# Attention plus maxout experts on one core: reordered first loads, one store per output tile, and column tiles for the last 64 queries

## The chip, the cores and the metric

The kernel runs on one core of a Trainium2 chip. The metric is the device time of one execution in microseconds (us). The kernel before the change takes 385.0 us (median; 383.74 to 385.46). "Ratio" below is the mean time of one kernel's fast runs over the mean of the other's of the same rounds, so it is not quite the ratio of the medians that are quoted; the bracket after it is its 95% interval. "Faster" or "slower" means by more than 2%.

Names used: PE is the matrix engine and PEld its weight load; ACT, DVE and POOL are the scalar, vector and general engines; SPq is the queue of SyncE, which issues nearly all transfers. "exp" is one ACT instruction, on 128x1024 elements in 312 of the 336 cases and on fewer in the rest.

## The reference, cut to what matters

```python
# q, k, v: [B=8, H=8, S=1152, D=64] float32
q_pool = q.reshape(B, H, S // 2, 2, D).mean(axis=3)            # 576 queries
scores = (1 / sqrt(D)) * q_pool @ k.transpose(0, 1, 3, 2)
attn = exp(scores - max) / sum                                 # softmax over 1152 keys
x = (attn @ v).transpose(0, 2, 1, 3).reshape(4608, 512)
g = maximum(x @ w1, x @ w2)                                    # [4608, 1024]
out = g @ w_out                                                # [4608, 512] float32
```

## The kernel before

The kernel is written as its own scheduler. `Plan` holds a planned clock for every engine. Jobs (transposes, attention products, expert products) offer *units* to PE, and a loop picks the next unit by planned times. The result is one fixed instruction order for each engine, and PE runs it in that order. So each planned cost (`cost=`) decides the order, and a wrong one can show as a wait on the chip.

Work is done for pairs of heads, 32 pairs in all. Scores for a pair use two row tiles of PE (64 contraction rows each). The attention-value product has the exponentials `et` as stationary operand and `vE` (64 values and a column of ones) as the moving one, so 65 columns stream for each 128 queries. 576 queries are four and a half chunks of 128: the last 64 queries were padded to 128 columns.

```python
def chunk(half, sb):                       # half: head of the pair; sb: 0..4
    def go(e, m):
        for t in range(NT):                # 9 key blocks
            a = (half * 2 + es) * PW + t * SQ + sb * P
            last = e.matmul(fb[m][:, sb*66:sb*66+65], et[:, a:a + P],
                            vE[vs][:, t, half, 0:65], start=(t == 0), stop=(t == NT-1))
        return last
    return unit(need, 0.275, go)
# norm(half): one reciprocal [128 x 5], one multiply [128 x 5 x 64] into xnat
return [Job("a", [chunk(half, sb) for sb in range(NCH + 1)], norm(half), nb=i) for half in range(2)]
```

The expert part transposes x (`xT`) by transfers for most batches, by PE for the first and the last (`X_PE = (0, B - 1)`), computes `h` jobs (four matmuls of 512 columns each) and `p` jobs (twelve), and stores tiles of 128 tokens. Token order inside a tile is two groups of 64 rows, and each group lands in rows of `out` that are nine apart:

```python
def store(lo, s):                                   # before: two transfers per tile
    for half in range(2):
        n0 = lo + half * HP                         # HP = 64
        b, at = n0 // SQ, n0 % SQ
        if b % 2: at = (at - NB) % SQ
        op("SP", lambda e, b=b, u=at // HP, half=half: e.dma_start(
            out[b*SQ:(b+1)*SQ, :].rearrange("(p u) e -> u p e", u=QU)[u, :, :],   # 64 x 512
            osb[s][rows(half), :]), r=[f"osb{s}"], dma=f"d_o{s}", cost=0.4)
```

The planned cost of an exp is `0.24 + n/700` for n columns of a head, 0.971 us for the usual 512. Bursts of scores hold 2 or 3 exps' worth; the third is allowed while the expert backlog is over 600 tokens (`LAG`).

The softmax here doesn't subtract the row's maximum and nothing guards it: scores larger than these inputs give would overflow.

Of the kernel before, what the change touches and what calls it, by code (L numbers as in the profile page):

```python
# [7 lines left out]
P = 128  # L8
# [7 lines left out]
class Plan:  # L16
# [29 lines left out]
    def when(self, eng, r=(), w=(), after=()):  # L46

        t = self.free.get(eng, 0.0)
        for d in self.deps(r, w, after)[0]:
            p = self.ops[d]  # L50
            if p["eng"] != eng or p["dma"] is not None:
                t = max(t, p["seen"] + 0.05)
        return t

    def op(self, eng, fn, r=(), w=(), dma=None, cost=0.1, mode="f", after=(), solo=False):
# [9 lines left out]
        if dma is not None:  # L65
            self.free[eng] = t + (1.3 if mode == "t" else 0.5)
            self.dma_free = max(self.free[eng] + 1.2, self.dma_free) + cost
            seen = self.dma_free + 0.7
        else:
            if eng == "PE" and mode != self.mode:  # L70
                t += 0.1
                self.mode = mode
            self.free[eng] = t + cost
            seen = t + cost + self.LAT[eng]
# [9 lines left out]
    def solve(self):  # L84
# [3 lines left out]
        for n, o in enumerate(ops):  # L88
# [3 lines left out]
            for d in sorted(o["deps"], reverse=True):  # L92
                p = ops[d]
                if p["dma"] is None:
                    if p["eng"] == eng and (eng == "PE" or d not in o["raw"]):
                        continue
# [57 lines left out]
def bass_funnel_attn__then__act_maxout2_kernel(  # L154
# [32 lines left out]
    with ctx:  # L187
# [10 lines left out]
        qp = [sbuf([HP, QU, 2, D], BF16, f"qp{s}") for s in range(2)]  # L198
# [4 lines left out]
        et = sbuf([P, 4 * PW + HP], BF16, "et")  # L203
        et2 = et[:, 0:4 * PW].rearrange("p (h c) -> p h c", h=2)
# [25 lines left out]

        def setup():
# [5 lines left out]
            def ones(g):  # L237
                g.memset(et[:, 4 * PW:], 0.0)
# [4 lines left out]
            op("POOL", ones, w=["vE0", "vE1", "vE2", "pad"])  # L243

        def load_k(i, lo=0, hi=NT):
            b, h0, s = i // NHP, 2 * (i % NHP), i % 3
            op("SP", lambda e: e.dma_start(
                kraw[s][:, :, lo:hi, :],
                k[b, h0:h0 + 2, :, :].rearrange("h (p t) d -> p h t d", t=NT)[:, :, lo:hi, :]),
                w=[f"kraw{s}"] if hi == NT else [f"kraw{s}.0"], dma=f"d_k{s}" if hi == NT else "d_k",  # L250
                cost=1.5 * (hi - lo) / NT)

        def load_q(i):
            b, h0, s = i // NHP, 2 * (i % NHP), i % 3
            for half in range(2) if i == 0 else (None,):
                at = slice(0, P) if half is None else rows(half)
                hs = slice(h0, h0 + 2) if half is None else slice(h0 + half, h0 + half + 1)
                op("SP", lambda e, at=at, hs=hs: e.dma_start(
                    qraw[s][at, :, :, :].rearrange("p u r d -> p (u r d)"),
                    q[b, hs, :, :].rearrange("h (p r) d -> (h p) (r d)", p=HP)),  # L260
                    w=["qraw0.0"] if half == 0 else [f"qraw{s}"],
                    dma="d_q" if half == 0 else f"d_q{s}", cost=1.45 if half is None else 0.75)
# [8 lines left out]
        def cast_k(i):  # L271
# [4 lines left out]
                w=[f"kbf{s}"] + (["kbf0.0", "kbf0.3"] if i == 2 else []), cost=1.13)  # L276

        def cast_k0(lo, hi, part):
            op("ACT", lambda e: e.activation(
                kbf[0][:, lo:hi, :, :].rearrange("p t h d -> p h t d"), kraw[0][:, :, lo:hi, :],  # L280
                COPY), r=[part], w=[f"kbf0.{lo}"], cost=0.2 + (hi - lo) * 0.092)
# [10 lines left out]

        def cast_q(i):
            s, r = i % 2, i % 3
            for half in range(2):
                a = qraw[r][rows(half), :, :, :]
                op("DVE" if i == 0 else "POOL", lambda g, half=half, a=a: g.tensor_tensor(  # L297
                    qp[s][:, :, half, :], a[:, :, 0, :], a[:, :, 1, :], ALU.add),
                    r=["qraw0.0" if i == 0 and half == 0 else f"qraw{r}"], w=[f"qp{s}.{half}"], cost=0.65 if i == 0 else 1.4,
                    solo=i > 0 and half == 1)  # L300

        def cast_v(i):
# [3 lines left out]
                1.0, 1.0, ALU.mult, ALU.mult), r=[f"vraw{r}"], w=[f"vE{r}"], cost=1.13)  # L306

        def unit(r, cost, go, mode="f"):
# [3 lines left out]
            return r, plan_it, cost  # L312
# [4 lines left out]
        def qtrans(i):  # L317
# [10 lines left out]
            def evac(m):  # L328
                mb = fb[m][:, :].bitcast(BF16)
                dve(lambda e: e.tensor_copy(qpT[i % 3][:, :], mb[:, 0:SQ]),  # L330
                    [f"f{m}"], [f"qpT{i % 3}", f"f{m}"], 0.4)
            return Job("q", [unit([f"qp{s}.0", f"qp{s}.1", "ident"], 0.3, go, "s")], evac, ("q", i))

# [7 lines left out]
        def ktrans_pe(i, cuts=(0, 5, 9)):  # L341
# [3 lines left out]
            for lo, hi in zip(cuts, cuts[1:]):  # L345
# [8 lines left out]
                def evac(m, lo=lo, hi=hi):  # L354
# [4 lines left out]
                        [f"f{m}"], kkeys(i, lo, hi) + [f"f{m}"], 0.1 + (hi - lo) * 0.12)  # L359
# [5 lines left out]
        def av_jobs(i):  # L365
# [5 lines left out]
            need = [f"et{es}.{g - first(i)}" for g in range(first(i), after(i))] + [f"vE{vs}", "pad"]  # L371

            def chunk(half, sb):

                def go(e, m):
                    for t in range(NT):
                        a = (half * 2 + es) * PW + t * SQ + sb * P
# [5 lines left out]

            def norm(half):
                def evac(m):
                    c = c0 + half * D
                    a = fb[m][:, 0:(NCH + 1) * 66].rearrange("p (j c) -> p j c", c=66)
                    dve(lambda e: e.reciprocal(rc[half][:, :], a[:, :, 64:65]),  # L388
                        [f"f{m}"], [f"rc{half}"], 0.19)
                    dve(lambda e: e.tensor_tensor(  # L390
                        xnat[xs][:, :, c:c + D], a[:, :, 0:D],
                        rc[half][:, :].unsqueeze(2).to_broadcast([P, NCH + 1, D]), ALU.mult),
                        [f"f{m}", f"rc{half}"],
                        [f"xn{xs}.{h0 + half}", f"f{m}"], 0.5)
                return evac

            return [Job("a", [chunk(half, sb) for sb in range(NCH + 1)], norm(half), nb=i)
                    for half in range(2)]
# [21 lines left out]
        def skeys(g):  # L420
            return [key for i, t, *_ in pieces(g) for key in (f"kT{i % 3}.{t}", f"qpT{i % 3}")]

        def scores(g):
# [10 lines left out]
            def exp(a, z, keys):  # L434
# [3 lines left out]
                    r=[f"s{r}"], w=keys + [f"s{r}"], cost=0.24 + (z - a) / 700.0)  # L438
# [20 lines left out]
        def under(n0, n1):  # L459

            keys = [key for key, lo, hi in (("w2b", 512, 1536), ("w2T", 1536, 2560),
                                            ("w2f", 2560, NTOK)) if n0 < hi and lo < n1]
            if "w2T" in keys:
                keys += [f"w2T{ct}" for ct in range(NC_)]
            return keys

        def xsize(j):
            return P if j < NCH else NB

        def xtrans(b):  # L470
            xs = b % 2
            assert b == 0 or not queue["w"]
            for j in range(NCH + 1):
# [3 lines left out]
                    r=[f"xn{xs}.{h}" for h in range(H)], w=xkeys(n0, n0 + n),  # L477
                    after=under(n0, n0 + n), dma=f"d_x{xs}{j}", cost=0.65, mode="t")

        def xtrans_pe(b):  # L480
            xs = b % 2
            jobs = []
            for j in range(NCH + 1):
# [14 lines left out]
                jobs.append(Job("x", [unit([f"xn{xs}.{h}" for h in range(H)] + ["ident"],  # L498
# [15 lines left out]
        def w_cast(part, ct):  # L514
            if part == 0:
                dve(lambda e: e.tensor_copy(w2b[:, ct, :], w2f[:, ct, :]),
                    [f"w2f{ct}"], [f"w2b{ct}", "w2b"], 0.6)
            elif part == 1:
                dve(lambda e: e.tensor_tensor(  # L519
                    wd[:, ct, :], w1f[:, ct, :], w2f[:, ct, :], ALU.subtract),  # L520
                    [f"w1f{ct}", f"w2f{ct}"], [f"wd{ct}", "w2f"], 1.2)
            else:
                dve(lambda e: e.tensor_copy(  # L523
                    wo[:, 2 * ct:2 * ct + 2, :], wof[:, 2 * ct:2 * ct + 2, :]),
                    [f"wof{ct}"], [f"wo{2 * ct}", f"wo{2 * ct + 1}"], 0.6)

        def w2t_job(ct):
# [7 lines left out]
            def evac(m):  # L535
# [3 lines left out]
                    [f"f{m}"], [f"w2T{ct}", "w2T", f"f{m}"], 1.15)  # L539
            return Job("w", [unit([f"w2b{ct}", "w2b", "ident"], 0.44, go)], evac)  # L540
# [19 lines left out]
        def store(lo, s):  # L560

            for half in range(2):
                n0 = lo + half * HP
                b, at = n0 // SQ, n0 % SQ
                if b % 2:
                    at = (at - NB) % SQ
                op("SP", lambda e, b=b, u=at // HP, half=half: e.dma_start(
                    out[b * SQ:(b + 1) * SQ, :].rearrange("(p u) e -> u p e", u=QU)[u, :, :],
                    osb[s][rows(half), :]), r=[f"osb{s}"], dma=f"d_o{s}", cost=0.4)
# [4 lines left out]
        def h_jobs(nb, tail):  # L574
# [4 lines left out]
            for ft in range(NF):  # L579
# [6 lines left out]
                def evac(m, ft=ft):  # L586
# [5 lines left out]
                    else:  # L592
                        dve(lambda e: e.tensor_scalar_max(  # L593
                            gT[:, ft, g0:g0 + size], fb[m][:, 0:size], 0.0),
                            [f"f{m}"], w, 0.1 + size / 960.0)
# [3 lines left out]
        def p_job(lo, tail):  # L599
            hi = lo + P  # L600

            def part(j):
                def go(e, m):
# [5 lines left out]
                    return e.matmul(fb[m][:, :], lhs, rhs, start=(j == 0), stop=(j == NC_ + NF - 1))  # L609
                if j < NC_:  # L610
                    return unit([f"w21{j}"] + xkeys(lo, hi), 0.216, go)
                return unit([f"wo{j - NC_}", f"gT.{lo % RING // P}.{j - NC_}"], 0.216, go)

            def evac(m):
                o = ocount[0] % 4
# [6 lines left out]
                else:  # L622
                    dve(lambda e: e.tensor_copy(osb[o][:, :], fb[m][:, :]),  # L623
                        [f"f{m}"], [f"osb{o}", f"f{m}"], 0.63)
                held[o] = (lo, o)
            return Job("p", [part(j) for j in range(NC_ + NF)], evac, nb=hi)
# [11 lines left out]
        p_got = set()  # L638
        p_at = [0]
# [53 lines left out]
        def start_w(n):  # L693
            for ct in range(NC_):
                load("w", (n, ct), got_w, f"{('w2f', 'w1f', 'wof')[n]}{ct}")

        def got_w(at):
# [3 lines left out]
            def ready():  # L701
# [3 lines left out]
                elif n == 2 and ct == NC_ - 1:  # L705
# [18 lines left out]
        def flush():  # L724
# [24 lines left out]
            for b in list(x_wait):  # L749
# [3 lines left out]
                elif plan.ops[plan.writer[f"xn{b % 2}.{H - 1}"]]["seen"] <= now():  # L753
# [15 lines left out]
        def burst_size():  # L769

            done = [b for b in range(B) if all(av_half.get(b * NHP + j) == 2 for j in range(NHP))]
            return 3 if len(done) * SQ - p_end[0] > LAG else 2

        def more_moe():
# [10 lines left out]
            while p_at[0] + P <= h_end[0] and f"w21{NC_ - 1}" in plan.writer:  # L785
                queue["p"].append(p_job(p_at[0], tail))
# [58 lines left out]
        def emit_unit(kk):  # L845
# [17 lines left out]
            elif job.kind == "p":  # L863
                p_got.add(job.nb)
                while p_end[0] + P in p_got:
                    p_end[0] += P
            if job.done:
# [7 lines left out]

        setup()
        load_q(0)
        load_k(0, 0, 3)
        load_k(0, 3, NT)
        cast_k0(0, 3, "kraw0.0")  # L880
        cast_q(0)
        cast_k0(3, NT, "kraw0")
        queue["q"].append(qtrans(0))
        queue["k"].extend(ktrans_pe(0, (0, 3, NT)))
        load_k(1)
        load_q(1)
        load_v(0)
        cast_k(1)
        queue["k"].extend(ktrans_pe(1))
        cast_q(1)  # L890
        queue["q"].append(qtrans(1))
        cast_v(0)
        load("k", 2, load_k, "kraw2")
        load("q", 2, load_q, "qraw2")
# [98 lines left out]
```

## Time and profile before

| | before |
|---|---|
| time, median | 385.0 us |
| span in the profile | 382.8 us |
| PE busy | 363.7 us, 95% |
| ACT busy | 316.9 us, 83% |
| mean DMA rate | 231 GB/s |

Two stretches of the same kernel. Columns: stretch, length, then busy us (and count) of PE, PEld, DVE, ACT, POOL, then granted PE clock, DMA share, GB/s.

```profile
20.00:40.00 20.00, 16.43 (x334) 11.76 (x333) 12.09 (x24) 18.93 (x23) 11.41 (x9) 1.00 1.04 396
...
200.00:220.00 20.00, 20.00 (x293) 12.01 (x293) 6.01 (x13) 18.88 (x22) 9.41 (x9) 1.00 1.11 309
```

Early on ACT leads (18.93 of 20 us); from about 60 us to 340 us PE has almost no gaps.

Two of the waits (total us, times, longest), and two steps of PE in order of time (start, us, what):

```profile
POOL qp L297 <- DMA qpT<-qp: 21.3, 13, 4.3
...
PEld sps L429 <- ACT et L436: 15.3, 37, 0.8
```

```profile
120.47 0.83 PE L429 MATMUL sps<-qpT,kT 64*128 64x320 bf16 x12
...
121.23 1.53 PE L378 MATMUL fb<-vE,et 128*128 128x65 bf16 x45
```

The 45 matmuls of the second step are one head's five chunks of nine; single records in it start 29 ns apart.

### The profile page before, as it was taken

The numbers are of one execution on the slowest core, as the hardware profiler recorded it, in microseconds if no ns is written. First come the engines' busy times: TensorE is split into PE (matmuls) and PEld (weight loads), VectorE is DVE, ScalarE is ACT, GpSimd is POOL, SyncE is SP. The second block draws the span as 40 slices with busy tenths as digits, with TensorE's granted clock in tenths as the row PEclk, the third lists the DMA queues.
The fourth block names the chain that finished last, engine by engine and source line by source line (L and its number), as shares of the span: only waits on it lengthen the run. The fifth ranks groups of instructions, "written<-read, shape, count | busy, mean of one in ns | idle before, by whom it ended". The sixth has DMA issues, their size and how long they took to land.

```text
span 382.8 us, 11318 instructions
## 1 busy us (share of the span) xinstructions
PE 363.7 (95%) x5010; PEld 210.8 (55%) x5010; DVE 140.2 (37%) x283; ACT 316.9 (83%) x355; POOL 162.0 (42%) x135
## 2 busy tenths in 40 slices
PE   2787999999999999999999999999999999999995
PEld 1365546555555555455556565555455655667642
DVE  2274934442234223422252224422442244237201
ACT  3998989999999999999999999999899999902210
POOL 1955597665554555555453535545545110000000
PEclk9999999999999999999999999999999999999999
DMA  8999999999989998999799999999899460121144
GB/s 248 405 391 399 392 257 312 331 309 312 225 234 295 273 272 174 309 320 275 142 265 289 319 179 212 286 258 315 200 236 267 94 109 14 29 44 42 29 95 98
DMA packets 93521, 88.58 MB, mean 231 GB/s; under 512 B 66080, under 2 KB 66592, under 8 KB 93472
## 3 DMA queue, kind: packets, MB, share of 16 engines
q1 hardware_dynamic: 93472, 87.86, 89.4%
q8 instruction: 39, 0.64, 0.7%
q14 instruction: 10, 0.08, 0.1%
HBM read 62.91 MB, written 9.44 MB: 189 GB/s over the span
## 4 chain that ended last, share of the span: by engine, by line
PE 85%; DMA 6%; DVE 4%; POOL 2%; issue 1%; SPq 1%; POOLq 0%
PE fb L378 22%; PE fb L609 21%; PE sps L429 18%; PE fb L582 15%; PE sps L609 4%; DMA qraw<-in_q_dram 3%; DMA kraw<-in_k_dram 2%; PE sps L582 2%; DVE wd L519 2%; POOL qp L297 1%; PE fb L547 1%; DVE xnat L390 1%; POOL vE L304 1%; PE fb L489 1%; DVE wo L523 1%
## 5 line engine op out<-in xcount | busy, mean ns | idle before, releaser
L436 ACT ACTIVATE et<-sps 128x1024 bf16<-128x1024 f32 (+1 forms) x336 | 307.8, 1005 | 19.0 <-PE sps L429 17.2
L378 PEld LDWEIGHTS fb<-vE,et 128*128 128x128 bf16 x2880 | 93.4, 97 | 20.9 <-issue 10.9
L378 PE MATMUL fb<-vE,et 128*128 128x65 bf16 x2880 | 101.9, 193 | 0.3
L297 POOL TENSOR_TENSOR qp<-qraw 64x576 bf16<-64x576 f32 x62 | 88.6, 1429 | 30.6 <-DMA qpT<-qp 21.3
L429 PE MATMUL sps<-qpT,kT 64*128 64x512 bf16 (+7 forms) x1152 | 96.9, 289 | 3.0 <-ACT et L436 2.1
L304 POOL TENSOR_SCALAR vE<-vraw 128x1152 bf16<-128x1152 f32 x32 | 36.9, 1152 | 103.2 <-PE fb L378 95.8
L429 PEld LDWEIGHTS sps<-qpT,kT 64*128 64x128 bf16 x1152 | 41.8, 95 | 51.3 <-issue 19.6
L582 PE MATMUL fb<-xT,wd 128*128 128x512 bf16 (+3 forms) x276 | 63.1, 360 | 0.7 <-DVE stage L623 0.7
L609 PE MATMUL fb<-wo,stage 128*128 128x512 bf16 x240 | 62.4, 380 | 0.0
L593 DVE TENSOR_SCALAR stage<-fb 128x512 bf16<-128x512 f32 (+3 forms) x64 | 41.9, 657 | 32.3 <-PE fb L582 32.1
L388 DVE RECIPROCAL rc<-fb 128x5 f32<-128x5 f32 x64 | 12.4, 194 | 112.3 <-PE fb L378 112.3
L273 POOL TENSOR_SCALAR kbf<-kraw 128x1152 bf16<-128x1152 f32 x31 | 36.2, 1167 | 14.6 <-DMA kraw<-in_k_dram 12.5
L582 PEld LDWEIGHTS fb<-xT,wd 128*128 128x128 bf16 x276 | 22.8, 98 | 29.4 <-DVE stage L593 6.3
L623 DVE COPY stage<-fb 128x512 f32<-128x512 f32 x29 | 20.0, 690 | 50.2 <-PE fb L609 49.7
L609 PEld LDWEIGHTS fb<-wo,stage 128*128 128x128 bf16 x240 | 21.1, 97 | 23.3 <-issue 3.3
L390 DVE TENSOR_TENSOR xnat<-fb,rc 128x320 bf16<-128x320 f32 x64 | 31.5, 491 | 2.2
L609 PE MATMUL fb<-w,xT 128*128 128x512 bf16 x120 | 32.1, 380 | 0.0
L609 PEld LDWEIGHTS fb<-w,xT 128*128 128x128 bf16 x120 | 10.3, 98 | 11.7 <-issue 2.0
L589 ACT ACTIVATE stage<-sps 128x256 bf16<-128x256 f32 (+1 forms) x7 | 2.3, 338 | 16.4 <-PE sps L582 16.4
L620 ACT COPY stage<-sps 128x512 f32<-128x512 f32 x3 | 1.8, 585 | 13.8 <-PE sps L609 13.8
L609 PE MATMUL sps<-wo,stage 128*128 128x512 bf16 x48 | 11.3, 379 | 0.0
L582 PE MATMUL sps<-xT,wd 128*128 128x256 bf16 (+2 forms) x76 | 10.3, 275 | 0.0
(40 smaller groups left out, 96.4 us busy)
## 6 DMA issues: line engine op xcount, KB each, us to landing
vraw<-in_v_dram SPq DMA_DIRECT2D x32, 576.0 KB, 7.7
kraw<-in_k_dram SPq DMA_DIRECT2D x31, 576.0 KB, 6.6
qraw<-in_q_dram SPq DMA_DIRECT2D x31, 576.0 KB, 5.8
out_dram<-stage SPq DMA_DIRECT2D x72, 128.0 KB, 2.4
xT<-in_moe_w_dram SPq DMA_DIRECT2D x4, 512.0 KB, 11.9
stage<-in_moe_w_out_dram SPq DMA_DIRECT2D x4, 512.0 KB, 14.2
stage<-in_moe_w_dram SPq DMA_DIRECT2D x4, 512.0 KB, 13.2
qraw<-in_q_dram SPq DMA_DIRECT2D x2, 288.0 KB, 4.1
```

Source lines behind the costliest of these rows:

```text
L273: op("POOL", lambda g: g.tensor_scalar(kbf[s][:, :, :, :].rearrange("p t h d -> p h t d"), kraw[r][:, :, :, :], 1.0, 1.0, ALU.mult, ALU.mu ...
L297: op("DVE" if i == 0 else "POOL", lambda g, half=half, a=a: g.tensor_tensor(qp[s][:, :, half, :], a[:, :, 0, :], a[:, :, 1, :], ALU.add), ...
L304: op("POOL", lambda g: g.tensor_scalar(vE[r][:, :, :, 0:D].rearrange("p t h d -> p h t d"), vraw[r][:, :, :, :], 1.0, 1.0, ALU.mult, ALU.m ...
L378: last = e.matmul(fb[m][:, sb * 66:sb * 66 + 65], et[:, a:a + P], vE[vs][:, t, half, 0:65], start=(t == 0), stop=(t == NT - 1))
L388: dve(lambda e: e.reciprocal(rc[half][:, :], a[:, :, 64:65]), [f"f{m}"], [f"rc{half}"], 0.19)
L390: dve(lambda e: e.tensor_tensor(xnat[xs][:, :, c:c + D], a[:, :, 0:D], rc[half][:, :].unsqueeze(2).to_broadcast([P, NCH + 1, D]), ALU.mult ...
L429: last = e.matmul(sps[r][:, h, col:col + hi - lo], kT[i % 3][rows(h), t, :], qpT[i % 3][rows(h), lo:hi], start=True, stop=True)
L436: op("ACT", lambda e: e.activation(et2[:, :, c:c + z - a], sps[r][:, :, a - g * W:z - g * W], EXP, scale=scale), r=[f"s{r}"], w=keys + [f" ...
L582: return e.matmul(fb[m][:, 0:size], wd[:, ct, ft * P:(ft + 1) * P], xT[:, ct, n0:n1], start=(ct == 0), stop=(ct == NC_ - 1))
L593: dve(lambda e: e.tensor_scalar_max(gT[:, ft, g0:g0 + size], fb[m][:, 0:size], 0.0), [f"f{m}"], w, 0.1 + size / 960.0)
L609: return e.matmul(fb[m][:, :], lhs, rhs, start=(j == 0), stop=(j == NC_ + NF - 1))
L623: dve(lambda e: e.tensor_copy(osb[o][:, :], fb[m][:, :]), [f"f{m}"], [f"osb{o}", f"f{m}"], 0.63)
```

## The change

The change has four intentions:

1. The last 64 queries of the two heads of a pair, padded to 128 columns before, run as two *column tiles*: each stationary block has 64 columns and sits in one half of PE's columns, so the two heads' products can run at the same time.
2. An output tile is stored with one transfer instead of two; the last tile is split by columns, 384 and 128.
3. The first loads are reordered and cut differently (q in two pieces, k whole).
4. The planned costs and the choice of units are adjusted: exp `0.05 + n/600` (0.903 us for 512), longer bursts of scores, other ranks, and a rule that places the column-tile unit next to a change of tile mode.

```diff
+            def rest():
+                def go(e, m):
+                    for t in range(NT):
+                        for half in range(2):
+                            a = col(half, t, NCH)
+                            last = e.matmul(
+                                fb[m][rows(half), NCH * 66:NCH * 66 + 65], et[:, a:a + NB],
+                                vE[vs][:, t, half, 0:65], start=(t == 0), stop=(t == NT - 1))
+                    return last
+                return unit(need, 0.275, go, "c")
 ...                                        # norm(0) gets two multiplies of 64x64, both multiplies shrink
-            return [Job("a", [chunk(half, sb) for sb in range(NCH + 1)], norm(half), nb=i)
-                    for half in range(2)]
+            return [Job("a", ([] if half else [rest()]) + [chunk(half, sb) for sb in range(NCH)],
+                        norm(half), nb=i) for half in range(2)]
 ...
-                    r=[f"s{r}"], w=keys + [f"s{r}"], cost=0.24 + (z - a) / 700.0)
+                    r=[f"s{r}"], w=keys + [f"s{r}"], cost=0.05 + (z - a) / 600.0)
 ...
-        def store(lo, s):
-            for half in range(2):
-                ...                        # two transfers, 64 x 512 each (shown above)
+        def store(lo, s, c0=0, c1=E, eng="SP"):
+            b, at = lo // SQ, lo % SQ
+            u = at // HP if b % 2 == 0 else (at - NB) // HP
+            if u == QU - 1:
+                to = out[b * SQ:(b + 2) * SQ, c0:c1].rearrange("(b p u) e -> u b p e", b=2, u=QU)[u]
+            else:
+                to = out[b * SQ:(b + 1) * SQ, c0:c1].rearrange("(p u) e -> u p e", u=QU)[u:u + 2]
+            op(eng, lambda e: e.dma_start(to, osb[s][:, c0:c1]), r=[f"osb{s}"],
+               dma=f"d_o{s}" if eng == "SP" else "d_z", cost=0.75 * (c1 - c0) / E)
 ...
-            return 3 if len(done) * SQ - p_end[0] > LAG else 2
+            return 3 if done else 2
 ...
-        rank = {"q": 6, "k": 6, "x": 5, "a": 4, "w": 3, "p": 2, "h": 1}
+        rank = {"q": 6, "k": 6, "x": 5, "h": 5, "a": 4, "w": 3, "p": 1}
 ...
+            turn = [c for c in fresh if lane[c[3]].units[0][3] == "c"]
+            if turn and plan.mode == "s":
+                emit_unit(turn[0][3])
+                continue
+            if len(turn) < len(fresh) and plan.mode == "f":
+                fresh = [c for c in fresh if c not in turn]
 ...                                        # first loads, weight order, DVE costs, split of the last tile
```

## The prediction

> **What bounds the kernel now.** One core, granted clock 1.00. The page gives PE 363.7 us busy of a 382.8 us span (95%), ACT 83%, DVE 37%, and the chain of waits is 85% PE. Window sums show PE busy 16.4 of 20 us in 20–40 us, 18.9 in 40–60, then 49.3 to 50.0 of every 50 us until 340. So there are two regimes. Until about 60 us the exponentials lead (ACT 18.9 of 20 us, one 128x1024 exp every 0.90 us at best), because no expert work exists before the first batch is complete. After that the in-order PE stream is the limit, and ACT has slack: the last 275 exps take 0.977 us each against 0.903 at best.
>
> **Costs read from single records.** Attention-value matmuls (65 columns) start every 29 ns; a 512-column matmul every 216 ns. Every change between 128-row and 64-row tile mode adds 95 to 99 ns over streaming, in 250 cases. [...] Adding these up gives 326 us of streaming, 262 mode changes (25 us), and about 30 us without work: 19.6 us of it before 60 us, about 0.5 us per 20 us later, 1.7 us at the end.
>
> **What the change does.**
> 1. Per head pair, 18 padded 128-column matmuls become 18 half-width ones in two column tiles. Streaming falls from 90 to 81 slots per pair: 288 slots x 29 ns = 8.4 us less, if a pair costs one slot. Scores already do this with row tiles: partners start 4 ns apart and a 64-column pair takes 29 ns, loads included. No column tile runs before. [...] At 60 ns the saving is gone.
> 2. The instruction order shows the third mode costs changes: 293 instead of 262, +31 x 97 ns = +3.0 us. Longer score bursts already offset part of it.
> 3. First loads: q in two pieces, k whole, first cast and transpose of one block instead of three (ACT 0.52 us, DVE 0.36 us each shrink). First exp at 8.9 us now; I expect 8.2 to 8.7. The order of later k loads should remove a 1.0 us ACT wait at 36 us. All this is on the path in the ACT-led stage: about -1 us. Earlier weight preparation moves work into idle PE but expert work starts at the same exp (59th instead of 60th), so I give it nothing.
> 4. Stores: 72 become 37. In the stream that is free. At the end, one issue instead of two, and the last tile split 384/128 so its eviction (0.69 us) shrinks: -0.8 us.
> 5. DVE gets two small multiplies per pair (+0.3 us, estimate from the 0.49 us multiply) and more self-waits: off the path at 37%.
>
> **Sum.** -8.4 +3.0 -1.0 -0.8 = -7.2 us: about 377.6 us against 385.0. I expect the pair to be concurrent (3 in 4). Predicted 377.5 us, range 373.5 to 383. Faster by over 2% 0.48, within 2% 0.50, slower 0.02.
>
> **What would show it.** Column-tile partners starting a few ns apart, pairs about 29 ns apart, rest unit about 0.27 us; 95–100 ns at each change; first exp before 8.7 us; PE still over 98% busy from 60 to 340 us; last exp earlier than 334 us (about 325), longer expert tail.
>
> **What would make it wrong.** Weight loads of column tiles that serialise (pair 55 ns or more: about 385 us). The plan's exp cost is now the best case (0.90 us), so the in-order PE may wait for ACT. Upwards in gain: better-calibrated costs could remove some of the 0.5 us stalls per 20 us, and freeing early PE could start experts sooner.

## More of the kernel before

From the page of the kernel before: busy time by engine; the busy tenths of PE, the granted PE clock and the DMA share in 40 slices; the queue that carries nearly all transfers (packets, MB, share of 16 engines' span); the chain of waits; the attention-value group; the stores (count, KB each, us from issue to landing).

```profile
PE 363.7 (95%) x5010; PEld 210.8 (55%) x5010; DVE 140.2 (37%) x283; ACT 316.9 (83%) x355; POOL 162.0 (42%) x135
...
PE   2787999999999999999999999999999999999995
...
PEclk9999999999999999999999999999999999999999
DMA  8999999999989998999799999999899460121144
...
q1 hardware_dynamic: 93472, 87.86, 89.4%
...
PE 85%; DMA 6%; DVE 4%; POOL 2%; issue 1%; SPq 1%; POOLq 0%
...
L378 PE MATMUL fb<-vE,et 128*128 128x65 bf16 x2880 | 101.9, 193 | 0.3
...
out_dram<-stage SPq DMA_DIRECT2D x72, 128.0 KB, 2.4
```

Two things matter. PE leads: it is busy 95% of the span and is 85% of the chain of waits. And the transfer engines have little to spare: packets of the main queue fill 89.4% of the span of all 16, and the DMA row stays at 7 to 9 tenths for the first 31 of 40 slices.

The rate of 396 GB/s at a share of 1.04 is an estimated 25 GB/s for each of 16 engines (396 / 16), a number that is needed later.

## The result, and the profile after

The changed kernel takes 455.91 us (median of four runs; 453.96 to 461.17, of which the 461.17 is a slow run), ratio 1.1822 [1.1758, 1.1886]: 71 us longer, where 7 us shorter was predicted. The granted clock averages 0.935 in the profiled run.

The same lines of the page after the change, and the group of the column tiles:

```profile
PE 368.0 (81%) x4990; PEld 210.6 (46%) x5040; DVE 150.5 (33%) x350; ACT 315.8 (70%) x356; POOL 161.2 (36%) x133
...
PE   3889999995598897694998669993996999997940
...
PEclk9999999998699999697999969997999999998985
DMA  8999899989799959999979969999989920011111
...
PE 40%; DMA 27%; SPq 11%; POOL 8%; issue 4%; ACT 4%; DVE 2%; POOLq 0%; DVEq 0%
...
L415 PE MATMUL fb<-vE,et 128*128 128x65 bf16 x2232 | 80.7, 194 | 1.5 <-DVE xnat L447 0.8
...
L427 PE MATMUL fb<-vE,et 128*64 128x65 bf16 x558 | 14.7, 197 | 0.0
...
out_dram<-stage SPq DMA_DIRECT2D x35, 256.0 KB
```

PE has about as much work as before (368.0 us) but is no longer what the kernel waits for: its share of the chain fell from 85% to 40%, and transfers with the queue that issues them make up 38%. Its row has holes throughout, and the clock row dips with them. The last eight slices of the DMA row show the oddest thing: the transfer engines do almost nothing, and the kernel is not over.

Stretches of after, columns as before:

```profile
200.00:220.00 20.00, 13.38 (x196) 7.46 (x197) 5.03 (x11) 12.24 (x15) 4.61 (x4) 0.83 1.09 151
436.00:450.00 14.00, 0.00 (x0) 0.00 (x0) 0.29 (x1) 0.00 (x0) 0.00 (x0) 0.60 0.13 50
```

In the second stretch PE, ACT and POOL are finished and only stores run: a DMA share of 0.13 of 16 engines, which is 2.1 engines, at 50 GB/s. In the first, the engines report a share of 1.09 as before, but move 151 GB/s instead of 309.

The longest waits of after, then four steps of the chain of waits in order of time:

```profile
POOL qp L314 <- DMA qpT<-qp: 103.2, 16, 15.6
...
PE fb L640 <- DMA xT<-xnat: 32.0, 5, 9.0
...
PE sps L486 <- DMA kT<-kbf: 9.8, 2, 6.4
```

```profile
176.58 8.51 DMA kT<-kbf
...
200.89 3.38 SPq L534
...
204.31 2.43 SPq L534
...
208.11 1.76 SPq L534
```

The transposing transfers of q, x and k are late, and line 534, SyncE issuing the x transposes, is itself slow (a median of 1.63 us for each issue, 1.27 before). Meanwhile the column tiles look as intended:

```profile
69.07 0.61 PE L486 MATMUL sps<-qpT,kT 64*128 64x64 bf16 x8
...
69.61 0.47 PE L427 MATMUL fb<-vE,et 128*64 128x65 bf16 x18
...
70.01 1.26 PE L415 MATMUL fb<-vE,et 128*128 128x65 bf16 x36
```

Eighteen half-width matmuls take the 0.40 us from 69.61 to 70.01, change of mode included. In single records partners start 3 ns apart and the next pair 30 ns after the second partner, so it is 33 ns from pair to pair (medians). So the loss was looked for in the stores, or in something else that delays transfers; the experiments were to say which.

### The profile page after: what moved, and what is told of

Same layout as the page of the kernel before. It is cut to its first block, busy times and chain, and to the rows that moved or that the text cites. A ratio compares the mean times of both kernels' runs of the same rounds, so it can differ in the third digit from the quotient of the medians.

```text
span 453.1 us, 11363 instructions
## 1 busy us (share of the span) xinstructions
PE 368.0 (81%) x4990; PEld 210.6 (46%) x5040; DVE 150.5 (33%) x350; ACT 315.8 (70%) x356; POOL 161.2 (36%) x133
## 4 chain that ended last, share of the span: by engine, by line
PE 40%; DMA 27%; SPq 11%; POOL 8%; issue 4%; ACT 4%; DVE 2%; POOLq 0%; DVEq 0%
PE fb L667 9%; PE fb L640 9%; PE sps L486 9%; DMA qraw<-in_q_dram 8%; PE fb L415 8%; SPq L534 5%; DMA xT<-xnat 5%; DMA out_dram<-stage 5%; POOL qp L314 4%; DMA kT<-kbf 4%; DMA kraw<-in_k_dram 4%; ACT et L493 4%; SPq L297 3%; PE sps L640 2%; SPq L370 2%
## 5 line engine op out<-in xcount | busy, mean ns | idle before, releaser
L640 PE MATMUL fb<-xT,wd 128*128 128x512 bf16 (+2 forms) x249 | 63.2, 390 | 33.7 <-DMA xT<-xnat 32.0
L415 PE MATMUL fb<-vE,et 128*128 128x65 bf16 x2232 | 80.7, 194 | 1.5 <-DVE xnat L447 0.8
L415 PEld LDWEIGHTS fb<-vE,et 128*128 128x128 bf16 x2232 | 72.8, 97 | 13.0 <-issue 5.5
L651 DVE TENSOR_SCALAR stage<-fb 128x512 bf16<-128x512 f32 (+2 forms) x60 | 40.3, 672 | 84.8 <-PE fb L640 83.6
L667 PE MATMUL fb<-wo,stage 128*128 128x512 bf16 x206 | 56.3, 391 | 1.1 <-issue 0.2
L437 DVE RECIPROCAL rc<-fb 128x5 f32<-128x5 f32 (+1 forms) x62 | 11.6, 188 | 91.8 <-PE fb L415 91.8
L447 DVE TENSOR_TENSOR xnat<-fb,rc 128x256 bf16<-128x256 f32 x62 | 26.3, 424 | 2.1
L667 PEld LDWEIGHTS fb<-w,xT 128*128 128x128 bf16 x112 | 10.3, 101 | 12.2 <-issue 2.8
L667 PE MATMUL sps<-wo,stage 128*128 128x512 bf16 (+2 forms) x71 | 15.3, 355 | 0.1
L427 PEld LDWEIGHTS fb<-vE,et 128*64 128x64 bf16 x558 | 11.3, 111 | 7.6 <-issue 6.5
L427 PE MATMUL fb<-vE,et 128*64 128x65 bf16 x558 | 14.7, 197 | 0.0
```

Source lines behind the costliest of these rows:

```text
L415: last = e.matmul(fb[m][:, sb * 66:sb * 66 + 65], et[:, a:a + P], vE[vs][:, t, half, 0:65], start=(t == 0), stop=(t == NT - 1))
L427: last = e.matmul(fb[m][rows(half), NCH * 66:NCH * 66 + 65], et[:, a:a + NB], vE[vs][:, t, half, 0:65], start=(t == 0), stop=(t == NT - 1))
L447: dve(lambda e: e.tensor_tensor(xnat[xs][:, 0:NCH, c:c + D], a[:, 0:NCH, 0:D], rc[half][:, 0:NCH].unsqueeze(2).to_broadcast([P, NCH, D]), ...
L640: return e.matmul(fb[m][:, 0:size], wd[:, ct, ft * P:(ft + 1) * P], xT[:, ct, n0:n1], start=(ct == 0), stop=(ct == NC_ - 1))
L651: dve(lambda e: e.tensor_scalar_max(gT[:, ft, g0:g0 + size], fb[m][:, 0:size], 0.0), [f"f{m}"], w, 0.16 + size / 960.0)
L667: return e.matmul(fb[m][:, 0:c1 - c0], lhs, rhs[:, c0:c1], start=(j == 0), stop=(j == NC_ + NF - 1))
```

## The experiments

Eighteen runs followed the result (e7 and e10 are the same kernel; e2, e4 and e7 were timed twice, the others four or six times). e1 to e4, e5 to e8, e9 to e12, the f runs at 0.22 and 0.20, and f_col_14 with g1 are five groups, each timed in its own rounds. In every group the kernel before was run beside them (medians 384.36 to 384.73 us). All outputs are right.

| run | what | median us | ratio [95%] |
|---|---|---|---|
| after | the change | 455.91 | 1.1822 [1.1758, 1.1886] |
| e1 | after, two stores per tile again | 386.75 | 1.0043 [1.0005, 1.0081] |
| e2 | before, one store per tile | 459.56 | 1.1959 [1.1920, 1.1999] |
| e3 | e1 without column tiles | 387.89 | 1.0096 [1.0076, 1.0115] |
| e4 | after, stores issued by ACT's queue | 464.60 | 1.2090 [1.2060, 1.2120] |
| e5 | e1, batch 1's x transposed by PE | 382.65 | 0.9956 [0.9941, 0.9971] |
| e6 | e1, old planned exp cost | 395.92 | 1.0308 [1.0273, 1.0342] |
| e7 | e1, old bursts and ranks | 382.36 | 0.9946 [0.9927, 0.9966] |
| e8 | e1, x transposes issued first | 383.46 | 0.9979 [0.9964, 0.9994] |
| e9 | e7 without column tiles | 385.39 | 1.0028 [0.9988, 1.0069] |
| e10 | e7 again | 384.69 | 0.9994 [0.9936, 1.0052] |
| e11 | e7, planned exp cost 0.08 + n/600 | 384.41 | 0.9992 [0.9963, 1.0021] |
| e12 | before with column tiles | 387.47 | 1.0072 [1.0044, 1.0101] |
| f_before_22 | before, planned exp 0.22 + n/700 | 383.32 | 0.9967 [0.9939, 0.9995] |
| f_before_20 | before, 0.20 + n/700 | 384.91 | 1.0006 [0.9983, 1.0029] |
| f_col_22 | e12, 0.22 + n/700 | 391.69 | 1.0177 [1.0154, 1.0199] |
| f_col_20 | e12, 0.20 + n/700 | 383.61 | 0.9968 [0.9947, 0.9988] |
| f_col_14 | e12, 0.14 + n/700 | 389.85 | 1.0141 [1.0120, 1.0162] |
| g1 | e1 with e5 and e8 | 382.88 | 0.9963 [0.9925, 1.0001] |

### Where the 71 us come from (e1 to e4)

**The theory.** The destination of the one-piece store is "two groups of 64 rows of 512", so its outermost dimension is 2. The theory is that such a store is carried by 2 of the 16 engines. The trace of after shows it: 2.1 engines are busy at 50 GB/s when nothing else runs. The updates of semaphores in the trace of after show it store by store: each of its 32 two-group stores on SyncE posts three updates, one about 1 us after issue and two close together 9.9 us after issue (median; 7.7 at best). Every load posts 16, and so do the four one-piece stores whose rows are equally spaced (128 rows outermost); the least disturbed of these four landed in 2.3 us. One transfer of 256 KB is thus not slow by itself. That the size of the outermost dimension sets the number of engines is the reading; no run varied it alone. The rivals: the order of the queue (a store that waits for its tile holds up the loads behind it on SyncE), and the column tiles or the new order of work.

**e1** undoes the store alone:

```diff
-            op(eng, lambda e: e.dma_start(to, osb[s][:, c0:c1]), r=[f"osb{s}"], ...)
+            for half in range(2):
+                if u == QU - 1:
+                    to = out[(b + half) * SQ:(b + half + 1) * SQ, c0:c1].rearrange(
+                        "(p u) e -> u p e", u=QU)[u]
+                else:
+                    to = out[b * SQ:(b + 1) * SQ, c0:c1].rearrange("(p u) e -> u p e", u=QU)[u + half]
+                op(eng, lambda e, to=to, half=half: e.dma_start(to, osb[s][rows(half), c0:c1]), ...)
```

> The changed kernel with one part undone: each 128-row tile is stored as two 64-row transfers again; loads, column tiles and plan constants stay. Theory (the one-piece store, whose outermost dimension in DRAM has size 2, is carried by 2 of the 16 DMA engines: in the last 25 us of the changed kernel 2.1 engines are busy at 51 GB/s): 375 to 381 us, clock 1.00, stores land in about 2.4 us again, no wait of PE for the transposed x. Rival A (the plan's optimistic exp cost makes PE and ACT wait for each other): stays above 420 us. Rival B (column tiles or longer idle gaps make the clock throttle, which costs the time): clock stays near 0.93 and time above 420 us.

Measured: 386.75 us, ratio 1.0043. The store was worth 69 of the 71 us. The first stretch is back at PE 19.88 of 20 us and 290 GB/s; columns as before:

```profile
200.00:220.00 20.00, 19.88 (x288) 10.95 (x290) 7.67 (x19) 19.01 (x22) 10.38 (x9) 1.00 1.12 290
```

**e2** puts the one-piece store alone into the kernel before (the `store` of the change, full tiles only).

> The kernel before with only the one-piece store added. Theory: it alone makes the kernel slow: 435 to 465 us, with 2 engines busy in the drain at the end and the granted clock below 1.00 as a consequence of PE waiting. Rivals A and B (the cause lies in the plan constants or the column tiles): 383 to 388 us.

Measured: 459.56 us (two runs), ratio 1.1959. The store alone reproduces the whole loss, without column tiles and without the new order. The drain at its end shows the same two engines and the same rate:

```profile
440.00:455.00 15.00, 0.00 (x0) 0.00 (x0) 0.00 (x0) 0.00 (x0) 0.00 (x0) 0.50 0.13 51
```

**e4** leaves the change as it is but issues the stores from ACT's queue, so that nothing on SyncE stands behind them.

```diff
-        def store(lo, s, c0=0, c1=E, eng="SP"):
+        def store(lo, s, c0=0, c1=E, eng="ACT"):
 ...                                        # semaphore names follow
```

> The changed kernel with its one-piece stores all issued from ScalarE's queue, so that no load or transpose stands behind a store in the SyncE queue. Theory of capacity (two engines hold 31 of 36 tiles' bytes, about 8 MB at 51 GB/s, 155 us of work on top of their share of the loads): stays above 430 us. Theory of order (the harm is that SyncE blocks and loads queue behind stores): falls below 410 us, even with some 0.5 us of issue per store on ScalarE.

Measured: 464.6 us (two runs), ratio 1.2090, slower still. POOL's wait for q's transposes falls from 103 to 46 us, so the queue's order did delay something; but PE waits longer for the x transposes (38.5 us instead of 32.0), and the drain still moves 51 GB/s at a share of 0.13. The order of SyncE's queue is not what limits; the two engines stay slow wherever the stores are issued. The drain of e4, columns as before:

```profile
445.00:460.00 15.00, 0.35 (x7) 0.17 (x4) 0.29 (x1) 0.20 (x1) 0.00 (x0) 0.66 0.13 51
```

**e3** takes the column tiles out of e1 (padded chunk and single multiply restored, as in the kernel before).

> As e1, and the column tiles undone too (the last 64 queries of each head in a padded 128-column chunk again). The column tiles' worth is e3 minus e1. If my sum holds (288 slots of 29 ns saved, about 31 more mode changes of 97 ns): e3 is 5 to 6 us slower than e1, about 383 us. If the DVE work or the extra changes eat it: within 1 us of e1. If column tiles are harmful: e3 faster than e1.

Measured: 387.89 us, 1.1 us longer than e1 (medians; the intervals of the two ratios overlap). The tiles are not the loss; but they are not worth the 5.4 us predicted for them either. That opened the second question.

**How two engines cost 71 us.** The stores of 32 of the 36 tiles have the two-group form (the other four merge into 128 equally spaced rows). They are 32 x 262,144 bytes, 8.4 MB; at the measured 50 GB/s that is an estimated 168 us of work for the two engines alone. The page of before shows that packets already filled 89.4% of every engine's span on average. A load of q, k or v posts 16 updates and counts as landed with the last. In after the last two come late: the sixteenth follows the fourteenth by 1.7 us for q, 1.2 for k and 0.5 for v on average, against 0.4, 0.4 and 0.3 before. That two of the 16 lag fits two busy engines, if each update is one engine's part; the trace does not name the engine of an update. So loads become late: the median from issue to landing rose from 6.6 to 9.2 us for k, from 5.8 to 8.9 for q and from 7.7 to 9.8 for v. The transposes rose too (k's from 6.5 to 8.4 us), but all their updates together, so that part is shown only by e1, which brings it back (6.9 us). The lines for k, before and then after (count, KB each, us from issue to landing):

```profile
kraw<-in_k_dram SPq DMA_DIRECT2D x31, 576.0 KB, 6.6
```

```profile
kraw<-in_k_dram SPq DMA_DIRECT2D x32, 576.0 KB, 9.2
```

Long waits of PE cost a second time. Seven times after the first loads PE waits for 3.0 us or more in after, and 1.8 to 5.1 us after the start of each of these waits the granted clock is halved, for 3.4, 6.8 or 10.2 us, 44.4 us in all. (Another 16.5 us lie in the drain, where PE has nothing to do; before has 1.8 us, all after its last matmul.) Split at PE's last matmul, 56.9 us of the loss come before it (it ends at 435.6 instead of 378.7 us) and 13.4 us after it, in the drain (17.5 instead of 4.1 us to the end).

### Why the repaired kernel is not 7 us faster (e5 to e12)

With two stores, everything else of the change should have given about 6.4 us (the prediction without its store term). e1 gives 1.7 us the other way. The sum over matmul records was put into a streaming model, which counts two partners in a row tile or column tile as one: a step in single records has a median of 56 ns for 128 columns, 109 for 256, 162 for 384 (after alone) and 216 for 512, which a fitted line of 2.5 ns + 0.417 ns per column meets to 1 ns, and of 29 ns for an attention-value product. e1 and the runs up to e12 lack some 50 records of expert matmuls of 512 columns, which the sums below add back at 216 ns each.

| | PE streaming, us | mode changes | the rest of the span, us |
|---|---|---|---|
| before | 326.5 | 262 | 31.0 |
| e1 | 317.4 | 295 | about 39.3 |

(A mode change was 93 to 99 ns in single records; the rest is the span less streaming and 97 ns for each change.) The streaming saved is 9 us in this model, near the 8.4 predicted, and 33 more changes cost 3.2 us, near the 3.0 predicted. But the model takes a pair of column tiles as one slot of 29 ns, and the records do not: from the first to the last start of a unit of 18 they show 281 ns, where 8 steps of 29 ns would be 232. For 32 units that is an estimated 1.6 us, which the table puts into "the rest". What failed is the last column: 8.3 us more, an estimated 6.7 of them with PE waiting or at half clock.

One hole is easy to see, between 110 and 120 us. The kernel before in this place, then e1:

```profile
110.00:115.00 5.00, 5.00 (x114) 3.65 (x114) 2.06 (x5) 4.42 (x6) 1.89 (x2) 1.00 0.97 293
```

```profile
110.00:115.00 5.00, 1.16 (x3) 0.58 (x5) 0.00 (x0) 1.77 (x2) 0.91 (x1) 0.86 0.48 100
115.00:120.00 5.00, 4.84 (x52) 2.78 (x52) 2.45 (x6) 2.51 (x3) 1.15 (x1) 0.80 0.87 200
```

```profile
113.84 1.06 PE L643 MATMUL fb<-xT,wd 128*128 128x512 bf16 x2 [4.37 <-DMA xT<-xnat]
```

PE waits 4.37 us for batch 2's x transposes and then runs 3.4 us at half clock. In the instruction order, no expert matmul stands between the 97th and the 107th exp: the backlog of expert work is used up. And the transposes were issued from 103.0 us on, behind another transfer that waited for a cast; before issued them at 95.6. The tiles do not make this hole: e3, which has no column tiles, waits at the same place, with a granted clock of 0.69 and 0.63 in the two stretches of 5 us from 105 us on. So e3 and e1 were compared with the hole in both.

```profile
107.86 1.87 PE L625 MATMUL fb<-xT,wd 128*128 128x512 bf16 x4 [3.23 <-DMA xT<-xnat]
```

**e5** transposes batch 1's x on PE instead of by transfers; **e8** moves the issue of x transposes to the front of the scheduler's loop, leaving PE's order unchanged:

```diff
-        X_PE = (0, B - 1)
+        X_PE = (0, 1, B - 1)                     # e5
```
```diff
         def flush():                             # e8: this loop stood at the end of flush()
+            for b in list(x_wait):
+                ...
+                    x_wait.remove(b)
+                    xtrans(b)
```

> e1 gave 386.8 us although its PE stream is shorter than that of before by 8.5 us of streaming less 3.2 us of mode changes; its trace has one hole between 100 and 117 us that the kernel before lacks (about 7 us without work or at half clock, first expert matmul of the second batch waits 4.4 us for the transposed x by DMA). Here the second batch's x is transposed on PE instead of by DMA. Theory (that hole gives the gain back; the x transposes land too late for the PE order): hole gone, 378 to 382 us (20 transposes and 4 to 5 evictions more, about 1.5 us). Rival (the hole only shows PE having nothing to do until the exponentials catch up; time is bound by ScalarE there): the idle time moves elsewhere, 385 to 388 us.

> e1 with the check for finished batches moved ahead of the check for finished casts, so that x transposes are issued on SyncE ahead of a q and a k transpose that wait for GpSimd; the order of PE is the same. Theory (x stands 6 us behind a k transpose that waits for a cast, at 97 to 103 us): x of the second batch issued near 98 us instead of 103, the hole shrinks by 4 to 6 us, 380 to 384 us. Rival (the SyncE order is not the cause): no change, 385 to 388 us.

Measured: e5 382.65 us and e8 383.46, that is 4.1 and 3.3 us less than e1 (an earlier group of rounds on the same chip). The hole was worth about that. e8 keeps the order of PE and so the stretch without expert matmuls, yet its clock stays at 1.00 there and the wait for x falls to 1.7 us at most: in e1 the late transpose did the harm, not the used-up backlog alone. **g1** has both and gives 382.88 (0.9963 [0.9925, 1.0001], six runs): the two repair the same hole and do not add.

> The best candidate: the changed kernel with two-piece stores (e1), x transposes ahead in the SyncE queue (e8) and the second batch's x transposed on PE (e5). No dry stretch in its order. Theory: 380.5 to 383 us, faster than both kernels by under 2%. If only e5's order was lucky: 383 to 386 us.

**e6** and **e7** undo the scheduling changes in e1: the planned exp cost, and the bursts and ranks.

```diff
-                    ..., cost=0.05 + (z - a) / 600.0)
+                    ..., cost=0.24 + (z - a) / 700.0)                              # e6
```
```diff
-            return 3 if done else 2
+            return 3 if len(done) * SQ - p_end[0] > LAG else 2                       # e7
-        rank = {"q": 6, "k": 6, "x": 5, "h": 5, "a": 4, "w": 3, "p": 1}
+        rank = {"q": 6, "k": 6, "x": 5, "a": 4, "w": 3, "p": 2, "h": 1}
```

> e1 with one constant of the plan put back: the exponential's planned cost 0.24 + n/700 us instead of 0.05 + n/600 (0.97 instead of 0.90 us for a full one; the trace of before has one start every 0.97 us on average from 60 us on). It changes only the order and interleaving. Theory (the plan runs ahead of the chip, so work is ordered before its data land): the 100 to 117 us hole shrinks below 3 us, 378 to 383 us. Rival (the hole comes from the exhausted backlog or from the order of the SyncE queue whatever the constant): 385 to 388 us.

> e1 with the burst rule (three score groups only with a backlog over 600 tokens) and the ranks of the job kinds of the kernel before. It has 298 mode changes instead of 295, and orders the second batch's expert work later (33rd expert matmul at the 110th exp instead of the 107th). Theory of a late x at one place: the hole shrinks, but less expert work fits beside the exponentials; 380 to 386 us. Rival (new burst rule and ranks are what costs e1 the gain): 377 to 380 us.

Measured: e6 395.92, 9.2 us worse than e1, with three dry stretches (10 exps or more without an expert matmul in the order: exps 89 to 101, 168 to 189, 290 to 303). So the new exp cost is not what hurts in e1; put back there, the old one is worse. e7 gave 382.36 in two runs, but its repetition **e10** on another chip, with four runs, 384.69 and an interval that includes 1. The gain of e7 did not repeat and is not claimed. **e9** (e7 without column tiles) gave 385.39 and **e11** (e7 with a planned exp cost of 0.933 us) 384.41; e9, e10, e11 and before cannot be told apart.

> e7 (no hole at 100 us) with the column tiles undone, to see their worth where the hole does not hide it. It has 268 mode changes against 298, and 288 more slots of 29 ns: my sum says 8.4 - 2.9 = 5.5 us slower than e7, near 388 us. If the shorter stream only turns into more waiting for ScalarE, the difference is below 2 us.

> The same kernel as e7, timed in the same rounds as the others, which its two runs before did not allow: 382 to 383 us, hole absent, clock 1.00 in the trace.

> e7 with the planned exponential 30 ns longer (0.93 us for a full one instead of 0.90; e7's trace has a start every 0.937 us on average). e7 has about 3.6 us in 17 waits of PE for the exponentials between 60 and 335 us, and the kernel before none. Theory (those waits come from the plan's best-case constant): they vanish, 379 to 382 us, less some 1.5 us for 15 more mode changes. Rival (any change of a constant reshuffles the whole order, as in e6, and the result is luck): anywhere from 381 to 395 us, with another late transfer.

**e12** goes the other way: the kernel before with column tiles (the `rest` unit, the two small multiplies, the rule that places the unit) and what goes with them. One part of that is a change of its own: DVE now waits for all of its own earlier instructions that it depends on, also those whose result it does not read. No run tests this alone, so for e12 and the f runs "column tiles" means both. (e3 and e9 keep it and undo the tiles alone.)

> The kernel before with the column tiles alone (its own loads, two-piece stores, constants, bursts and ranks). 302 mode changes instead of 260. My sum: -8.4 + 4.1 = -4.3 us, near 380.7 us. If the column tiles cost more than their stream shows (DVE multiplies, bank release): 384 us or above. If the whole order is upset by it as in e1: a hole with a late x near 100 us, 384 to 388 us.

Measured: 387.47 against 384.51 for before in the same rounds, ratio 1.0072 [1.0044, 1.0101]. Here column tiles lengthen the kernel although they shorten PE's stream.

### Is it the tiles or the order? (the f runs)

A change to the units changes the static order everywhere after it. To tell a cost of the tiles from luck in the order, the planned exp cost was varied with the tiles (on e12) and without (on before):

```diff
-                    r=[f"s{r}"], w=keys + [f"s{r}"], cost=0.24 + (z - a) / 700.0)
+                    r=[f"s{r}"], w=keys + [f"s{r}"], cost=0.22 + (z - a) / 700.0)   # or 0.20, 0.14
```

> The kernel before, with only the planned exponential 20 ns shorter (0.22 instead of 0.24 + n/700 us). The chip's work is the same; only the order of the instructions changes a little. Theory (the order of the kernel before is a lucky one among neighbours, and any change of the plan leaves it): 386 to 392 us. Rival (the order matters little; the column tiles themselves cost what they save): 384 to 386 us.

> The same with the planned exponential 40 ns shorter (0.20). Theory of the lucky order: 386 to 392 us. Rival: 384 to 386 us.

> The kernel before with column tiles alone (e12), planned exponential 0.22. Theory (column tiles save the 4.5 us that their records show: 0.407 us per unit with its mode change against 0.549 us for 18 slots; compared at equal plan constants and averaged over orders the saving shows): 3 to 6 us below f_before_22. Rival (waiting eats it at any order): within 1.5 us of f_before_22, or above.

> The same with 0.20, against f_before_20: 3 to 6 us below it by the theory; within 1.5 us or above by the rival.

> A fourth order of before with column tiles (planned exponential 0.14 + n/700 us). Counted in the instruction order, the kernels with a hole have a stretch of 10 or more exponentials in a row without one expert matmul: e1 and e8 from the 97th to the 107th, f_col_22 from the 258th to the 270th, e6 three such (12, 21 and 13 exps); the kernel before, f_before_22, f_before_20, e5, e7, e12 and f_col_20 have none. This order has none either and keeps more expert work for the end (441 of 784 expert matmuls done by the 300th exp, f_col_20 474 or so). Theory (a lighter attention stage lets the expert backlog run dry, and a dry stretch costs 4 to 10 us because PE then waits for ScalarE and falls to half clock): no hole, clock 1.00 from 60 us on, 381 to 384 us. Rival (column tiles cost time by themselves at any order): 385 us or more.

Measured, with the same sums (these traces lack no records):

| | median us | streaming, us | changes | the rest, us |
|---|---|---|---|---|
| f_before_22 | 383.32 | 326.2 | 258 | 30.4 |
| f_before_20 | 384.91 | 326.4 | 258 | 31.7 |
| f_col_22 | 391.69 | 317.5 | 302 | 43.9 |
| f_col_20 | 383.61 | 317.7 | 290 | 36.3 |
| f_col_14 | 389.85 | 317.6 | 292 | 42.3 |

Three readings follow. The streaming saved by the tiles is 8.7 us for 0.22 and for 0.20, the same in every order because the model counts slots; with pairs at their measured pace it is an estimated 1.6 us less. The added changes cost 3.1 to 4.3 us (32 to 44 times 97 ns). And the rest grows by 4.6 us (0.20) to 13.5 us (0.22): the net effect of the tiles on the time at the same planned cost was +3.0 us (e12 over before, medians of the same rounds), +8.4 us (0.22) and -1.3 us (0.20). The two pairs with the rule for DVE on both sides, e1 against e3 and e10 against e9, give -1.1 and -0.7 us, no more than the spread of their runs. Without tiles the kernel varies only from 383.3 to 385.0 over three costs, so before was not a lucky order among these.

Where f_col_22 loses is again a dry stretch, exps 258 to 270 in the order. f_before_22 in this place, then f_col_22 (stretches), then one step of its PE:

```profile
270.00:275.00 5.00, 5.00 (x54) 2.46 (x52) 2.77 (x4) 4.62 (x7) 3.50 (x3) 1.00 0.96 248
```

```profile
270.00:275.00 5.00, 2.61 (x44) 1.15 (x40) 0.61 (x2) 4.97 (x8) 4.03 (x4) 0.93 0.48 92
275.00:280.00 5.00, 5.00 (x82) 4.07 (x84) 1.06 (x4) 2.78 (x4) 1.03 (x1) 0.50 0.70 143
```

```profile
272.96 0.39 PE L451 MATMUL sps<-qpT,kT 64*128 64x192 bf16 x4 [0.53 <-ACT et L458]
```

PE has only scores left to issue, 0.39 us of them and then 0.53 us of waiting for ACT, and after some microseconds of that the clock is 0.50 for the next five.

f_col_14 was a miss. It was chosen because its order has no dry stretch, and its clock is indeed 1.00 after 60 us, but it takes 389.85 us, ratio 1.0141. Its planned exp cost, 0.871 us (0.14 + 512/700), is below the 0.903 us that the chip takes at best, and PE's weight loads wait for ACT more often than in f_col_20. The wait of f_col_14, then that of f_col_20 (total us, times, longest):

```profile
PEld sps L451 <- ACT et L458: 33.6, 99, 0.8
```

```profile
PEld sps L451 <- ACT et L458: 21.9, 54, 2.0
```

This suggests that a plan that thinks ACT too fast loses in many small waits. It is argued, not shown: PE's matmuls themselves wait for ACT no longer than in f_col_20 (4.2 against 4.9 us). Nor does a plan that thinks ACT too slow always run dry: e12 plans 0.971 us, has no dry stretch and still lost 3.0 us. The profiled run of f_col_14 was also at half clock for 10.2 us before 60 us; but its runs at mean clocks of 0.987 and 0.996 took 389.97 and 389.74 us, so that is not the loss either. A further part may be the normalisation: the two multiplies of 64x64 take 221 ns each, so 0.44 us per pair for both, and for one head of each pair the release of the bank waits for a reciprocal and three multiplies instead of one. The weight loads of the full chunks wait 5.9 us for the last multiply in f_col_20 (17 times), 2.5 us in f_before_20 (8 times).

No other planned costs were run without tiles. Which order keeps the saving of the tiles, and why most lose it, is left open.

## Why the prediction was wrong, point by point

**The step that failed is step 4: "Stores: 72 become 37. In the stream that is free."** It counted transfers and their issues, and not the engines that each one uses. The runs showed in its place: the one-piece store uses 2 of 16 engines (share 0.13 at 50 GB/s when alone), and this alone costs 69 us in the changed kernel (after against e1) and 75 us in the kernel before (e2). The prediction's list of what would make it wrong did not contain it. Part of the material was there beforehand: the new store's own pattern gives the destination as 2 x 64 x 512; the profile of before gives an estimated 25 GB/s per engine (396 / 16) and 89.4% of all engines' span already filled. What was missing is that such a store runs on two engines: the kernel before holds none, so its trace could not show it. With the two known, the stores are an estimated 168 us of work for them.

The other steps, read from e1 and the f runs, where the store no longer hides them:

1. Column tiles, "-8.4 us": about right as to PE's stream (partners 3 ns apart, but 33 ns from pair to pair where 29 were counted, so an estimated 7 us and not 8.4). Wrong as time. A unit of 18 takes 0.41 us with one change of mode, against 0.55 us for 18 padded slots, so each of 32 pairs of heads saves 0.14 us, 4.5 us in all. In time it came to between 1.3 us less and 8.4 us more at matched planned costs, because the order around the tiles had more waits. The prediction took every saved slot of PE as saved time, as "PE busy 95%" suggested.
2. Mode changes, "+3.0 us": right. 295 instead of 262 in e1 at 93 to 99 ns each, 3.2 us.
3. First loads, "-1 us", first exp between 8.2 and 8.7 us: wrong for the first exp, which begins at 9.27 us instead of 8.91. The lines of ACT's first cast and first exp, in before and then in e1:

```profile
6.42 0.52 ACT L279 ACTIVATE kbf<-kraw 128x384 bf16<-128x384 f32 x1 [4.36 <-DMA kraw<-in_k_dram]
...
8.91 3.77 ACT L436 ACTIVATE et<-sps 128x1024 bf16<-128x1024 f32 x4 [0.61 <-PE sps L429]
```

```profile
7.58 0.62 ACT L288 ACTIVATE kbf<-kraw 128x128 bf16<-128x128 f32 x2 [5.52 <-DMA kraw<-in_k_dram]
...
9.27 1.02 ACT L493 ACTIVATE et<-sps 128x1024 bf16<-128x1024 f32 x1 [1.07 <-PE sps L486]
```

   The cast of one block starts 1.2 us later, because it waits for the whole of k instead of its first third. The prediction costed the smaller cast and forgot the larger load. It varies: other profiles of kernels with the same start show the first exp from 8.2 (e5) to 10.3 us (e10). The later part of the step held: the timeline has the 45th exp beginning at 50.31 us before, and the record of e1 has it at 49.0 us, 1.3 us earlier.

4. The end, "-0.8 us": about right. From the last matmul to the end e1 takes 3.5 us, before 4.1.
5. DVE, "+0.3 us", "off the path at 37%": the two multiplies take 0.44 us a pair, and some of PE's waits are for them (5.9 against 2.5 us in the matched pair at 0.20), so not wholly off it.

With the store put right the sum would still have missed: 386.75 us (e1) against 377.5. The term that was mis-sized there is the one that the sum left at zero, PE's waits, which grew by an estimated 6.7 us (8.3 less the 1.6 of the pairs).

## What to carry to other kernels

Before merging transfers, read the shape on both sides as the instruction carries it. Here the stores with an outermost dimension of 2 ran on two engines (share 0.13 at 50 GB/s, three updates each), and those with 64 or 128 rows outermost posted all 16 updates; the issue that was saved cost 69 to 75 us. The first sign was late loads elsewhere, and the proof was the DMA share and rate in a stretch where nothing else ran. A shorter stream on the engine that leads is worth only what its order lets through: count its waits after the change as well as its work; here one of the best versions found, e5, is 0.4% faster than before (382.65 us, 0.9956 [0.9941, 0.9971]), which is within 2%; e5 was not repeated, and e7, which looked as good in the same rounds, was no faster than before when it was repeated.
